# Five of seven block products of two spans in a second level of Strassen, and the later norms' roots by logarithm and exponential

## The chip, the cores and the metric

The kernel runs on one core of a Trainium2 chip. The metric is device time in microseconds (us) of one execution; lower is better. The engines are TensorE (PE, with its weight loads listed as PEld), VectorE (DVE), ScalarE (ACT), GpSimd (POOL) and SyncE (SP), which issues most DMAs. Each works through its own instructions in the order in which the program lists them; semaphores hold an instruction until what it needs is there.

## The reference: what is computed

Attention with normalised queries and keys, then a feed-forward block, all in float32. Sizes: batch 8, 12 heads, 448 positions, head size 64; so 3584 tokens of 768, and a hidden size of 2048.

```python
def rmsnorm(x, g):
    rms = np.sqrt(np.mean(x * x, axis=-1, keepdims=True) + 1e-06)
    return x / rms * g
scores = scale * np.matmul(rmsnorm(q, g_q), rmsnorm(k, g_k).transpose(0, 1, 3, 2))
attn = np.exp(scores - max); attn = attn / (sum + 1e-9)
x = np.matmul(attn, v)            # -> tokens x 768
h = x @ w_in                      # 768 -> 2048
out = (np.maximum(h, 0.0) ** 2) @ w_out   # 2048 -> 768
```

## The kernel before, in words

**Spans.** Two batches make a span; there are four (NSPAN). The attention of span 0 runs first, alone (`attention_alone`, L917). Then each span has its first product (`first_product`, L1034: x @ w_in and the activation) and its second product (g @ w_out). Spans 0, 1 and 2 use `second_product` (L1091), span 3 uses `last_product` (L1144).

**Strassen.** Both products of a span are done in one level of Strassen over the two batches and the two halves of each dimension: seven block products instead of eight, named A11, A12, S2, S1, S3, A22, S4. The seven sums of weights are made once and kept in DRAM (`w1s`, `w2s`). The seven sums of activations are made by `combine` (L1021) into `gC` and `gT`, and by `combine_x` (L903) into `xC` and `xT`. One block product of the second product has 3 blocks of 128 output rows (m = 0 to 2, HC), a depth of 8 times 128 (HF), and 448 columns (S): 24 matmuls of 128x128 by 128x448. The hardware profile keeps two records for each of these float32 matmuls. `last_product` already splits the first two row blocks of each block product by a second level of Strassen: seven half-size products, each 4 matmuls by 224 columns, and the third row block is done plainly.

**Order around the change.** The order of every engine is written by hand. `attention(first)` (L972) and `second_product` are generators. The loop at L1379 runs one attention step and then draws so many units from `second_product` (`total`, `done`, L1378 to L1382); a unit is one matmul of `second_product`. An attention pair (two heads; 12 pairs per span) has five steps, each ended by a `yield`:

- A (L976 to L996): scores of two key chunks, the values of the pair before, the other two scores (all PE work of a pair is here), exponentials on ACT, `add_up` 1 and `norm_by_squares(i + 2)` on DVE and POOL;
- B (L997 to L1001): `transposes(i + 1)` (DVE), the load of v;
- C (L1002 to L1009): `add_up` 2 and 3, `finish(i - 1)` (DVE), `squares(i + 3)` (ACT);
- D (L1010 to L1014): `fold(i)` (DVE), `combine_x(i - 1)` (POOL, for the span's second batch);
- E (L1015 to L1018): POOL issues the DMA of the sums' reciprocals to DRAM and the two that spread them over partitions (`spread`, L826).

`norm_by_squares` (L739) sums squares on DVE (L744), swaps neighbouring groups of 32 partitions by four small DVE copies (L747), and takes the power -1/2 on POOL (L750), which then scales q and k (L752). `fold` (L812) sums the exponentials (L817) and moves quarters by three small DVE copies (L820).

**PSUM.** There are eight banks. `scores` holds four (`ps_s`), `values` two (`ps_o`), and two are left to the products (`ps_m`): `bank()` (L460) hands them out in turn, so `second_product` fills one bank while DVE or ACT reads the other. `last_product`, which has no attention beside it, keeps its sums pa, pb, pc and pd in four different banks.

**Weights.** `load_blocks` (L651) streams weight tiles `sw` in the order of use, five buffers ahead, on SP's queue.

## Time and profile before

| what | value |
|---|---|
| runs | 1353.47 us median of 3 (1352.96, 1353.47, 1356.8) |
| the profiled execution | 1352.32 us, of which the span of its instructions is 1350.1 us |
| busy share of the span | PE 98%, PEld 50%, DVE 65%, POOL 46%, ACT 32% |
| granted TensorE clock | 0.999 |
| second products of spans 0, 1, 2, with attention | 265.0 to 457.7, 587.0 to 778.9, 908.0 to 1100.0 us |
| first products of spans 0 to 3 | 131 to 265, 457.7 to 587.0, 778.9 to 908.0, 1100 to 1226 us |
| last product | 1226 to 1350 us |

How to read it: a line such as L1106 is a line of the kernel. A group's mean in ns is the length of one record; matmuls overlap in the pipeline, so a row of matmuls is paced by the distance of their starts, which is shorter than one record. Idle time of an engine costs something only where the chain that ends last runs through it.

### The profile page before, as it was taken

The page shows a single profiled execution, that of the slowest core. Times are in us where ns is not written, and L with a number is a line of the kernel's source. Part 1 is how long each engine was busy: PE and PEld are TensorE (multiplying, and loading weights), DVE is VectorE, ACT ScalarE, POOL GpSimd, SP SyncE. Part 2 cuts the span into 40 slices and gives each one's busy share as a digit, 9 for nine tenths or more (in the row PEclk, how much of TensorE's full clock was granted, in tenths as well). Part 3 has the DMA queues.
Part 4 walks back from the last instruction along what each step waited for, and adds up shares of the span by engine and source line. Part 5 has one row for each costly group of instructions (what it writes and reads, how often), then busy time and mean ns, then how long its engine had stood idle before and what let it go on. Part 6 is the DMA issues. An engine that isn't in the chain of part 4 may idle for free.

```text
span 1350.1 us, 17275 instructions
## 1 busy us (share of the span) xinstructions
PE 1329.7 (98%) x5786; PEld 671.6 (50%) x5786; DVE 873.4 (65%) x1537; ACT 431.8 (32%) x681; POOL 619.4 (46%) x504
## 2 busy tenths in 40 slices
PE   8999999999999999999999999999999999999997
PEld 3333445444444455444444455544444445556887
DVE  6999788599987333568777623457878743336553
ACT  7886466433332011233333111223333201111000
POOL 5767533466564122646556212446656412422452
PEclk9999999999999999999999999999999999999999
DMA  9877999655686333345676432345665444431333
GB/s 241 225 217 200 314 360 333 181 131 107 135 151 129 101 87 88 101 114 114 143 146 123 114 97 87 90 112 125 130 123 126 105 102 135 134 88 53 114 101 58
DMA packets 413814, 190.15 MB, mean 141 GB/s; under 512 B 282388, under 2 KB 408724, under 8 KB 413716
## 3 DMA queue, kind: packets, MB, share of 16 engines
q1 hardware_dynamic: 406164, 180.21, 52.0%
q0 software_dynamic: 4736, 8.40, 2.4%
q8 instruction: 48, 0.79, 0.3%
q10 hardware_dynamic: 2816, 0.34, 0.2%
q14 instruction: 50, 0.41, 0.1%
HBM read 155.72 MB, written 33.16 MB: 140 GB/s over the span
## 4 chain that ended last, share of the span: by engine, by line
PE 89%; DVE 5%; ACT 2%; DMA 1%; issue 1%; POOL 0%; SPq 0%; POOLq 0%; DVEq 0%
PE ps L1106 29%; PE pd L1068 10%; PE pa L1068 10%; PE pc L1068 10%; PE sc L785 7%; PE pav L862 7%; PE pb L1068 5%; PE ps L1234 3%; PE pd L1206 2%; PE pc L1206 2%; PE pa L1206 2%; DVE gT L810 1%; PE pb L1206 1%; DVE rstd L715 1%; ACT gT L797 1%
## 5 line engine op out<-in xcount | busy, mean ns | idle before, releaser
L1106 PE MATMUL ps<-gT,sw 128*128 128x448 f32 x576 | 225.8, 543 | 0.0
L1044 POOL TENSOR_TENSOR gT<-gT 128x448 f32<-128x448 f32 x96 | 94.1, 982 | 284.8 <-ACT gT L1040 284.8
L750 POOL TENSOR_TENSOR half<-half,mhalf 128x28 f32<-128x28 f32 x36 | 175.3, 4869 | 74.6 <-DVE half L749 74.0
L1106 PE MATMUL ps<-gC,sw 128*128 128x448 f32 x432 | 170.1, 543 | 0.0
L1106 PEld LDWEIGHTS ps<-gT,sw 128*128 128x128 f32 x576 | 107.5, 190 | 113.9 <-issue 110.1
L1068 PE MATMUL pa<-xT,sw 128*128 128x448 f32 x384 | 155.0, 540 | 0.6 <-ACT p L1072 0.6
L1040 ACT ACTIVATE gT<-gT 128x448 f32<-128x448 f32 x96 | 55.3, 576 | 313.4 <-DVE gT L1083 313.4
L1106 PEld LDWEIGHTS ps<-gC,sw 128*128 128x128 f32 x432 | 80.6, 190 | 86.3 <-issue 83.2
L787 ACT ACTIVATE pr<-sc 128x896 f32<-128x896 f32 x87 | 77.5, 915 | 124.1 <-PE sc L785 124.1
L785 PE MATMUL sc<-qkT 64*64 64x448 f32 (+1 forms) x1152 | 109.8, 496 | 0.0
L1068 PEld LDWEIGHTS pa<-xT,sw 128*128 128x128 f32 x384 | 72.8, 190 | 72.7 <-issue 70.1
L583 POOL TENSOR_TENSOR gC<-gC 128x384 f32<-128x384 f32 x64 | 76.2, 1208 | 62.2 <-DVE gC L579 60.4
L1083 DVE TENSOR_TENSOR gT<-z,pd 128x448 f32<-128x448 f32 x32 | 19.8, 619 | 97.8 <-PE pd L1068 97.7
L1068 PE MATMUL pd<-xT,sw 128*128 128x448 f32 x192 | 77.9, 542 | 1.3 <-DVE z L1075 1.3
L1068 PE MATMUL pd<-xC,sw 128*128 128x448 f32 x192 | 77.5, 540 | 1.3 <-DVE gT L1083 1.3
L830 POOL DMA_DIRECT2D xT<-factors x72 | 38.0, 532 | 88.4 <-DMA factors<-square 56.8
L1068 PE MATMUL pb<-xC,sw 128*128 128x448 f32 x192 | 77.5, 540 | 0.1
L1068 PE MATMUL pc<-xC,sw 128*128 128x448 f32 x192 | 77.4, 539 | 0.0
L1068 PE MATMUL pc<-xT,sw 128*128 128x448 f32 x192 | 77.4, 539 | 0.0
L752 POOL TENSOR_TENSOR qk<-qk,half 128x448 f32<-128x448 f32 x72 | 75.9, 1074 | 2.8
L862 PE MATMUL rest<-pr,vt 64*64 64x448 f32 x348 | 72.7, 537 | 0.0
L862 PE MATMUL pav<-pr,vt 64*64 64x448 f32 x348 | 72.7, 537 | 0.0
(233 smaller groups left out, 2159.2 us busy)
## 6 DMA issues: line engine op xcount, KB each, us to landing
sw<-w1s SPq DMA_DIRECT2D x224, 192.0 KB, 2.4
sw<-w2s SPq DMA_DIRECT2D x126, 256.0 KB, 3.3
w1s<-gC SPq DMA_DIRECT2D x8, 1344.0 KB, 7.1
w2s<-gC SPq DMA_DIRECT2D x8, 1344.0 KB, 6.3
out_dram<-osb SPq DMA_DIRECT2D x184, 56.0 KB, 1.8
qk<-in_q_dram SPq DMA_DIRECT2D x144, 56.0 KB, 3.4
qk<-in_k_dram SPq DMA_DIRECT2D x144, 56.0 KB, 2.8
xT<-factors POOLq DMA_DIRECT2D x72, 112.0 KB, 3.4
```

Of the source, the lines that this page charges most:

```text
L583: nc.gpsimd.tensor_tensor(*[blocks_of(n)[:, place_of(n, i)] for i in (dst, x, y)], op)
L750: nc.gpsimd.tensor_tensor(half, half, mhalf, ALU.pow)
L752: nc.gpsimd.tensor_tensor(qkn[:, s], raw[:, s], half[:, s * NG:(s + 1) * NG].rearrange("p g -> p g ()").to_broadcast([P, NG, 32]), ALU.mult)
L785: nc.tensor.matmul(sc[part, h, 0:n], qkT[rows, 0, 1, keys], qkT[rows, 0, 0, of], start=True, stop=True)
L787: nc.scalar.activation(pr, sc[:, :, 0:n], AF.Exp)
L862: nc.tensor.matmul(into, vs[i][rows, h, c, :], probs[i, c][rows, h, :], start=(c == 0), stop=(c == NF), skip_group_check=True)
L1040: nc.scalar.activation(g, src, AF.Relu)
L1044: nc.gpsimd.tensor_tensor(g, g, g, ALU.mult)
L1068: nc.tensor.matmul(ps, stream[n + at][:, c], rhs[:, c], start=first and c == 0, stop=c == HC - 1, skip_group_check=not first)
L1106: nc.tensor.matmul(ps, stream[n][:, c % 4], rhs_of[i][:, c], start=c == 0, stop=c == HF - 1)
L1206: nc.tensor.matmul(ps, lhs[:, c], rhs[:, c], start=first and c == 0, stop=c == HK - 1, skip_group_check=not first)
L1234: nc.tensor.matmul(ps, weights_of(o, m, c // HK)[:, c % HK], rhs_of[i][:, c, part], start=c == 0, stop=c == HF - 1)
```

## The change

1. **Second products of spans 1 and 2** use a new generator, `outer_product`, in place of `second_product`. A11 and A12 stay as they are. In S2, S1, S3, A22 and S4 the first two row blocks go through a second level of Strassen, and the third is done in two column halves of 224 (`third`). The sums of activations for the second level (`add_g`, four of 128x896 per block product) go on DVE, those of weights (two in `add_weights`, and two changes of a11 and a12 in place) on POOL. A unit is now two matmuls by 224 columns or one by 448, and `total` is 140 in place of 160.
2. **PSUM.** The second level needs four sums, and two banks are there: `held` cuts each bank into two halves of 224 columns. pa and pb lie in one bank and pc and pd in the other. pc and pd are open at once; only the first matmul into pc has the start flag, which clears the bank for both.
3. **Norms after span 0's.** The power on POOL gives way to Ln and Exp on ACT and four small POOL operations (`roots_by_squares`). The copies of `norm_by_squares` and `fold` move from DVE to ACT, and what follows them is put into functions of its own that are called a step later (`scale_by_squares` in step B, `roots_by_squares` in step C, `factors_of` in step E).
4. The order of weight loads becomes a list made at the start (`plan`, `begins`). The weights of the second level are loaded in four tiles per block product into dead parts of xC, xT and gC (`load_set`).

```diff
+    plan, begins = [], {}
...
     def norm_by_squares(i):
...
-            nc.vector.tensor_copy(other[n * 32:(n + 1) * 32], half[m * 32:(m + 1) * 32])
+            nc.scalar.copy(other[n * 32:(n + 1) * 32], half[m * 32:(m + 1) * 32])
...
+    def roots_by_squares(i):
...
-        nc.gpsimd.tensor_tensor(half, half, mhalf, ALU.pow)
+        nc.scalar.activation(y, half, AF.Ln, scale=2.0 ** -63)
+        nc.scalar.activation(y, y, AF.Exp, scale=-0.5, bias=rebias)
+        nc.gpsimd.tensor_tensor(half, half, y, ALU.mult)
+        nc.gpsimd.tensor_tensor(half, half, y, ALU.mult)
+        nc.gpsimd.tensor_scalar(half, half, -0.5, 1.5, ALU.mult, ALU.add)
+        nc.gpsimd.tensor_tensor(half, half, y, ALU.mult)
...
     def fold(i):
...
-            nc.vector.tensor_copy(quarters[0:32, n], quarters[n * 32:(n + 1) * 32, 0])
+            nc.scalar.copy(quarters[0:32, n], quarters[n * 32:(n + 1) * 32, 0])
+
+    def factors_of(i):
...
+    def outer_product(work, span):
...
+        order = (A11, A12, S2, S1, S3, A22, S4)
...
+        def add_g(o, k):
+            if o < len(order):
+                (b11, b12), (b21, b22) = [[b.rearrange("p (r h) n -> p r h n", h=2) for b in row] for row in parts_of(o)]
+                t1, t2, t3, t4 = (t_of(o, k) for k in range(4))
+                dst, x, y = ((t1, b12, b11), (t2, b22, t1), (t3, b22, b12), (t4, b21, t2))[k]
+                nc.vector.tensor_tensor(dst, x, y, sub)
+
+        def add_weights(o):
+            if o < len(order):
+                a11, _, a21, a22, s1 = tiles[o]
+                nc.gpsimd.tensor_tensor(s1, a21, a22, add)
+                nc.gpsimd.tensor_tensor(a21, a11, a21, sub)
+
+        def run(ps, lhs, rhs, start=True):
+            for c in range(HK):
+                nc.tensor.matmul(ps, lhs[:, c], rhs(c), start=start and c == 0, stop=c == HK - 1, skip_group_check=True)
+                if c % 2:
+                    yield
...
+        held = [ps[:, h * HS:(h + 1) * HS] for ps in (bank("both"), bank("both")) for h in range(2)]
+        for o, i in list(enumerate(order))[2:]:
...
+            pa, pb = held[o % 2], held[1 - o % 2]
+            pc, pd = held[2], held[3]
...
+            def third(half, ps):
+                for c in range(HF):
+                    load_blocks(n + 5)
+                    nc.tensor.matmul(ps, stream[n + c // 4][:, c % 4], rhs_of[i][:, c, half],
+                                     start=c == 0, stop=c == HF - 1, skip_group_check=True)
+                    if c % 2 and c < HF - 1:
+                        yield
+                nc.vector.tensor_tensor(dst[2][:, half], base[2][:, half], ps, add)
+                if more is not None:
+                    nc.vector.tensor_tensor(more[2][:, half], more[2][:, half], ps, add)
+                yield
+
+            yield from run(pa, a11, of(b11))
+            nc.scalar.copy(z, pa)
+            nc.gpsimd.tensor_tensor(a11, s1, a11, sub)
+            if o != 5:
+                send(o)
+            if o == 2:
+                add_g(2, 3)
+            else:
+                add_g(o + 1, 0)
+            yield from third(left, pc)
+            load_set(o + 1 if o > 2 else len(order))
+            yield from run(pa, a12, of(b21), False)
+            nc.gpsimd.tensor_tensor(a12, a12, a11, sub)
+            send(o)
+            if more is None:
+                nc.vector.tensor_tensor(into[0][:, left], base[0][:, left], pa, add)
+            else:
+                nc.scalar.copy(into[0][:, left], pa)
+            add_g(o + 1, 1 if o > 2 else 0)
+            yield from run(pb, a11, of_t(t2))
+            nc.vector.tensor_tensor(z, z, pb, add)
+            if more is None:
+                nc.gpsimd.tensor_tensor(into[1][:, left], z, base[1][:, left], add)
+                nc.gpsimd.tensor_tensor(into[0][:, right], z, base[0][:, right], add)
+            yield from run(pc, s1, of_t(t1))
+            nc.vector.tensor_tensor(y, z, pc, add)
+            yield from run(pd, a21, of_t(t3), False)
+            if more is None:
+                nc.vector.tensor_tensor(into[1][:, right], base[1][:, right], pd, add)
+                nc.gpsimd.tensor_tensor(into[1][:, right], into[1][:, right], y, add)
+            else:
+                nc.vector.tensor_tensor(into[1][:, right], y, pd, add)
+            add_g(o + 1, 2 if o > 2 else 1)
+            yield from third(right, pa)
+            n += 2
+            add_weights(o + 1)
+            if leaves:
+                deliver(work, span, dst[2], 2 + col, t)
+            yield from run(pc, a12, of(b22), False)
+            nc.vector.tensor_tensor(into[0][:, right], into[0][:, right] if more is None else z, pc, add)
+            add_g(o + 1, 3 if o > 2 else 2)
+            yield from run(pd, a22, of_t(t4), False)
+            nc.vector.tensor_tensor(into[1][:, left], into[1][:, left] if more is None else z, pd, add)
...
+            if i + 2 < last:
+                scale_by_squares(i + 2)
...
+            if i + 2 < last:
+                roots_by_squares(i + 2)
...
+                factors_of(i)
                 nc.gpsimd.dma_start(sums["out"][i % 2], sums["square"][0:2 * S // 32, 1])
...
-            rest = second_product(work, span)
+            rest = (outer_product if span else second_product)(work, span)
...
-            total, done, most = HC * (7 * HF + 4) - 20, 0, 10 * NPAIR + 1
+            total, done, most = 2 * HC * HF + 5 * 22 - 18 if span else HC * (7 * HF + 4) - 20, 0, 10 * NPAIR + 1
```

## The prediction, made before the changed kernel ran

> **What bounds the kernel now.** I read the chain that ended last first, then the table by stage, then PE, DVE and POOL in order of time. The chain is PE from end to end:
>
> ```profile
> PE 89%; DVE 5%; ACT 2%; DMA 1%; issue 1%; POOL 0%; SPq 0%; POOLq 0%; DVEq 0%
> ```
>
> By stage (start:end, length; then busy us of PE, PEld, DVE, ACT, POOL), the second products of spans 1 and 2, which the change rewrites:
>
> ```profile
> 587.00:778.90 191.90, 191.90 (x1088) 89.88 (x1087) 145.41 (x286) 58.49 (x82) 99.03 (x75) 1.00 0.59 126
> ...
> 908.00:1100.00 192.00, 192.00 (x1088) 89.97 (x1087) 144.76 (x286) 58.47 (x82) 99.33 (x75) 1.00 0.55 120
> ```
>
> PE is busy in all of it, DVE in 76%, POOL in 52%. So fewer matmul columns shorten these stages as long as PE never has to wait there; a shorter POOL or ACT alone gains nothing. How the attention lies in it (PE in order of time, span 1):
>
> ```profile
> 643.64 1.73 PE L785 MATMUL sc<-qkT 64*64 64x448 f32 x16
> ...
> 647.82 1.31 PE L785 MATMUL sc<-qkT 64*64 64x224 f32 x16
> 649.06 9.29 PE L1106 MATMUL ps<-gC,sw 128*128 128x448 f32 x24
> ...
> 659.03 1.73 PE L785 MATMUL sc<-qkT 64*64 64x448 f32 x16
> ```
>
> A pair's PE work is one lump, 643.64 to 649.06 = 5.42 us, then only product matmuls until the next lump at 659.03: a pair takes 15.4 us. The second level exists already in span 3; PE there:
>
> ```profile
> 1244.25 6.18 PE L1234 MATMUL ps<-gT,wb 128*128 128x448 f32 x16
> 1250.26 1.68 PE L1206 MATMUL pb<-xT 128*128 128x224 f32 x8
> 1251.78 1.68 PE L1206 MATMUL pc<-xT 128*128 128x224 f32 x8
> ...
> 1260.96 6.18 PE L1234 MATMUL ps<-gC,qk 128*128 128x448 f32 x16
> ```
>
> 16 records by 448 columns take 6.01 us from start to start (0.3757 each), 8 by 224 take 1.515 (0.1893 each).
>
> **PE work saved.** A float32 matmul leaves two records. A block product now: 24 x 2 x 0.3757 = 18.03 us. After: seven half products of 4 matmuls and a third block of 16, 44 x 2 x 0.1893 = 16.66. Saved 1.37, ten times (five products, two spans): **13.7 us**. The product of span 3 above took 16.71, so this pace can be had. Floor: 1352.3 (the profiled execution's own time; its span is 1350.1) - 13.7 = 1338.6.
>
> **Norms and copies.** Per pair POOL loses the power (L750, mean 4869 ns) and gains four operations on 28 columns. The trace has none: from below DVE's 188 ns (L748), from above POOL's 658 ns by 224 columns (L1255), so 0.7 to 2.6 us. DVE loses seven copies (4 at 174, 3 at 339 ns, 1.7 us); ACT gains them at 0.17 to 0.53 us each (L747; L992) and Ln and Exp (216 and 307 ns, L725, L726): 1.7 to 4.2 us per pair, with ACT busy 58 of 192 us. PE does not wait in span 0's second product either (busy 192.70 of 192.70), so nothing of this is on the path: 0, at best 0.8 (192.7 against 191.9). Weight loads: the same bytes, SP's queue, no row of PE waiting for `sw` in these stages: 0. What ACT's copies can cost: they wait in ACT's order for a DVE sum, and the exponentials stand behind them; `fold`'s copies come some 4.6 units (3.5 us) before the next lump, and PE has 2.6 us of values before it needs the first exponential, so DVE has to be some 6 us late; from then on its lateness would be paid.
>
> **DVE.** Attention per pair from its rows: adds 2 x 1.06 + 2 x 0.65 (L810, L808), sums 1.10 + 1.08 (L817, L744), two transposes 1.23 (L761), `finish` 0.62 + 0.66, and 1.2 of small ones: 9.3 us. In the middle four products (S2 to A22, 88 units of a matmul's length each): 17 `add_g` at 1.08 (L1192 where alone), 33 reads of a 224-wide sum at 0.385 (L1276, L1280), 5 transposes out at 0.64: 34.3 us. The loop draws 140 units over 61 steps, 11.5 per pair: 4.5 us. Together 13.8 us per pair against PE's 11.5 x 0.757 + 5.42 = 14.1. Busy times are 4% under the sum of the rows (145.4 against 151 in this stage), so 13.3. DVE fits, but 11 of it falls outside the lump, where PE takes 8.7: DVE runs up to 3 us late there, and catches up in the lump.
>
> POOL also slows DVE. From DVE and POOL in order of time:
>
> ```profile
> 1270.46 1.29 POOL L1180 TENSOR_TENSOR xT<-wb 128x512 f32<-128x512 f32 x1
> 1270.51 2.19 DVE L1192 TENSOR_TENSOR xT<-gC,xT 128x896 f32<-128x896 f32 x1
> 1271.33 1.51 PEld L1206 LDWEIGHTS pa<-gC,qk 128*128 128x128 f32 x8
> 1271.51 1.68 PE L1206 MATMUL pa<-gC,qk 128*128 128x224 f32 x8
> 1271.82 2.00 POOL L1180 TENSOR_TENSOR xT<-xT,wb 128x512 f32<-128x512 f32 x1
> ```
>
> The DVE add doubles beside POOL's. Over the last product L1192 averages 1.35 against 1.08 (+25%, POOL busy 41%). But L900 (two inputs in SBUF) stays at 0.62 beside L752. DVE has 6.5 us per pair of such adds: 0 to 1.6 us more; I take 0.3, as most of them are attention's, whose rows did not grow. The Trainium skill (GPSIMD Engine Reference, section Specifications) says that POOL's SBUF interfaces are shared with VectorE and that instructions with two SBUF inputs contend. By that rule all 6.5 us would grow, and the sum would move toward the upper end of this range; L900 says not every pair of operations does.
>
> **The new wait.** pa and pb share one bank, pc and pd the other. Three times per product the next matmuls write the half beside one just finished: pb after pa, pd after pc, and pd after pc again. Before the matmuls may start, DVE has to read that half, if accesses of two engines to one bank are kept in program order whatever the columns. Before has no two sums in one bank, so the trace does not show this. From below 0. From above, the nearest row, a matmul that waits until DVE has read its bank (span 2's first product):
>
> ```profile
> 863.82 0.61 DVE L1075 TENSOR_TENSOR z<-p,pb 128x448 f32<-128x448 f32 x1
> ...
> 864.49 0.30 PEld L1068 LDWEIGHTS pd<-xT,sw 128*128 128x128 f32 x2 [0.63 <-DVE z L1075]
> ```
>
> The read ends at 864.43 and PE resumes within 0.06 to 0.15 us. Read starts come 0.20 us after PE could have gone on (1320.04 and 1320.24, L1206 and L1280). So one wait is 0.20 + 0.39 + 0.1 = **0.7 us with an idle DVE**, plus all that stands before the read in DVE's queue. I take the wait: that row is the nearest, and the framework that places the semaphores orders an engine's access to a bank behind another's. The Trainium skill (PSUM — Partial Sum Buffer, section on bank collisions) says that two engines on one bank and quadrant at once raise an error even at disjoint columns, and that semaphores are to guard whole banks. With that rule the upper bound holds; without it, the lower. The one clearing flag itself removes no instruction: 0.
>
> **One product by hand**, steps A to E as the loop places them, PE's lump at 0. S2: lump to 5.4; units 1 to 8 would end at 11.5. DVE: step A's add waits for the second exponential (2.8 after the lump's start), two operations, 5.0; B 1.5; transpose out and `add_g` 1.7; C 3.6; third block's read 0.4; D 1.1; then the read of pa, done at 13.7: PE stands **2.3** us. The next wait (pd after pc) comes after the second lump, DVE is prompt: **0.7**. After it DVE has B, a read, `add_g`, C, a read, D, E and the read of pc ahead of PE's next start, 9.3 us of work and 0.3 of waiting for PE, against eight units of PE, 6.1: **3.7** with the restart. Sum 6.7. S1, shifted by a step: 2.4, 0 (the lump covers it), 2.8: 5.2. Mean 6.0, times four products and two spans: 48. S4 has no `add_g` and mostly no attention: 3 x 0.7 x 2 = 4. Off for overlapping rows, 0.5 us per pair (1 per product): -8. Contention 0.3 per pair: 0.6 x 8 = +5. Waits together 49, less 13.7: **+35**. So 1352.3 + 35 = 1387.6 for the profiled execution; its median of runs lies 1.15 higher (1353.47 against 1352.32): **1389**.
>
> **Rivals.**
> *Prompt DVE.* Only the bare waits: 0.7 x 3 x 10 = 21, less a few under lumps, 19; -13.7: 1359. For it: DVE is 24% idle now. Against: 13.3 of 14.1 us when it matters.
> *No wait within a bank: faster.* Reads of one half do not hold the other half, or the lumps cover them; then the shortest cover is four units (3 us) and DVE is mostly in time: 1340 to 1349. It decides at 13.7 / 30 = 0.46 us per wait, under the 0.7 of an idle DVE. At or near that point the time is unchanged.
> *DVE and POOL hold each other.* Contention of 1.6 us per pair (2.5 more per product, 8 products: +20) and a11 late from POOL, whose queue stands behind DMA landings (17.7 us of waits in span 1): 1405 to 1425.
> *The change does not do what it says*: at 224 columns a weight load (190 ns) is as long as the matmul's step, so PE cannot go below 0.1893; at 0.1878 it would save 14.9 in place of 13.7. That is in the sum.
>
> **Numbers.** Forecast, waits of 4 to 8 us per product (1374 to 1404): 0.52. Prompt DVE (1355 to 1374): 0.16. Held by contention (above 1404): 0.18. No or covered wait: 0.10 faster, 0.04 unchanged. A change under 0.3% can't be told from none here. Range 1357 to 1413: the forecast, nearly all of the prompt case, half of the contention. Faster 0.10, same 0.04, slower 0.86.
>
> **What would show it.** Right: in the second products of spans 1 and 2 PE is idle before the runs into pb and pd, some 24 us per span, and what ended it are DVE's reads of pa and pc; each stage is about 191.9 - 6.9 + 24.5 = 209.5 us long; S2 to A22 take 22 x 0.757 + 1.9 lumps of 5.42 + 6 = 33 us each; 224-wide records start 0.189 us apart. POOL's power is gone, and span 0's second product still takes 192 us. Wrong: PE busy throughout in these two stages (no such wait), or idle there with POOL, ACT or a DMA as what ended it, or starts further apart than 0.19.

## The result, and the profile after

The changed kernel takes 1460.39 us (median of 4 runs, 1459.51 to 1468.63), the kernel before 1354.28 (4 runs): 1.0795 times as long, 95% interval 1.0752 to 1.0837. The forecast was 1389 and the range 1357 to 1413: the sign was right, the loss three times the one forecast (106 us for 35).

Read in the same order as before. The changed kernel's row of granted clock in 40 slices, and its chain:

```profile
PEclk9999999999999999998998999999898899999999
...
PE 77%; DVE 12%; ACT 3%; issue 3%; DMA 2%; SPq 1%; POOL 1%; DVEq 0%; POOLq 0%; ACTq 0%
```

The path now runs through DVE for 12%, and the clock drops in two stretches. They are the second products of spans 1 and 2. By stage (start:end, length; PE, PEld, DVE, ACT, POOL; granted clock):

```profile
588.90:832.20 243.30, 203.67 (x1292) 138.07 (x1289) 162.37 (x252) 82.83 (x185) 119.47 (x143) 0.92 0.44 98
961.90:1203.90 242.00, 203.23 (x1292) 137.53 (x1289) 161.73 (x252) 82.88 (x185) 119.68 (x143) 0.92 0.41 94
```

Each takes 50 us more than its 192.7 of before; of a profiled difference of 107.9 us (1460.23 against 1352.32) the two hold 99.8. DVE is busy in only two thirds of them. Cut finer, span 1:

```profile
588.50:631.00 42.50, 42.50 (x248) 19.50 (x244) 29.30 (x48) 22.94 (x52) 15.84 (x26) 1.00 0.66 154
...
660.00:681.00 21.00, 16.70 (x112) 12.34 (x112) 13.46 (x22) 7.23 (x17) 10.44 (x15) 0.91 0.24 48
681.00:702.00 21.00, 17.30 (x108) 12.73 (x109) 14.49 (x25) 7.49 (x17) 9.18 (x12) 0.83 0.49 120
...
811.00:832.90 21.90, 20.29 (x119) 17.02 (x118) 8.61 (x20) 0.88 (x2) 6.13 (x9) 1.00 0.30 61
```

A11 and A12 (first line) lose nothing, S2 to A22 lose idle time and clock, S4 (last line, no attention beside it) hardly anything. PE in order of time, in S2 of span 1; the bracket is the idle time before, and what ended it:

```profile
672.47 3.19 PE L1295 MATMUL both<-gC,sw 128*128 128x224 f32 x16
675.50 1.68 PE L1229 MATMUL both<-gC,xC 128*128 128x224 f32 x8
682.04 3.36 PE L1229 MATMUL both<-gT,xC 128*128 128x224 f32 x8 [4.87 <-DVE p L1343]
685.19 1.33 PE L1229 MATMUL both<-gC,xC 128*128 128x224 f32 x3
```

The second run into pc ends, and the run into pd waits 4.87 us for DVE's read of pc (L1343), as forecast in place. But then its eight records take 3.36 us where the eight before took 1.68: the clock is at half. What DVE did meanwhile:

```profile
666.73 1.09 DVE L832 TENSOR_TENSOR acc<-pr 128x896 f32<-128x896 f32 x1 [3.20 <-ACT pr L809]
...
670.41 0.39 DVE L1329 TENSOR_TENSOR xC<-xC,both 128x224 f32<-128x224 f32 x1 [1.59 <-PE both L1229]
670.72 1.16 DVE L783 STREAM_TRANSPOSE qkT<-qk 128x448 f32<-128x448 f32 x2
...
673.98 1.55 DVE L832 TENSOR_TENSOR acc<-acc,qkT 128x896 f32<-128x896 f32 x1
675.57 1.27 DVE L830 TENSOR_TENSOR acc<-acc,half 64x448 f32<-64x448 f32 x2
676.87 0.62 DVE L926 TENSOR_TENSOR half<-pav,half 128x448 f32<-128x448 f32 x1
677.52 1.21 DVE L928 TENSOR_TENSOR xT<-half,xT 128x448 f32<-128x448 f32 x1
...
680.80 0.33 DVE L849 TENSOR_REDUCE square<-quarters 32x28 f32<-32x112 f32 x1 [0.75 <-ACT quarters L842]
...
681.65 0.33 DVE L1343 TENSOR_TENSOR p<-p,both 128x224 f32<-128x224 f32 x1
```

In the lump before (first line) it had stood itself, 3.20 us for an exponential. It waited for PE (1.59 us), then did one pair's attention steps B to E in a row, and only then the read of 0.33 us for which PE stood. DVE's waits in this stage (us in all, times, longest):

```profile
DVE acc L832 <- ACT pr L809: 25.3, 7, 4.6
DVE ct L1299 <- PE both L1295: 12.0, 5, 5.1
DVE acc L832 <- ACT qkT L809: 7.0, 2, 4.1
```

32 us of this stage DVE waits for exponentials, in the lumps; in the kernel before it is 18.7 us in the same stage, and PE never waits. So PE and DVE **take turns**: DVE idles in the lump, PE behind it. Every span has 14 waits of PE, 39.6 and 38.7 us: three in each of S2, S3, A22 and S4, two in S1. Eight are long (2.7 to 6.4), six are near the bare wait for one read (0.48 to 0.57).

### The profile page after: what moved, and what is told of

The parts are those of the page before. It is cut to its first block, busy times and chain, and to the rows that moved or that the text cites. A ratio compares the mean times of both kernels' runs of the same rounds, so it can differ in the third digit from the quotient of the medians.

```text
span 1458.4 us, 18435 instructions
## 1 busy us (share of the span) xinstructions
PE 1354.4 (93%) x6186; PEld 768.5 (53%) x6186; DVE 883.6 (61%) x1371; ACT 507.7 (35%) x1017; POOL 610.3 (42%) x684
## 4 chain that ended last, share of the span: by engine, by line
PE 77%; DVE 12%; ACT 3%; issue 3%; DMA 2%; SPq 1%; POOL 1%; DVEq 0%; POOLq 0%; ACTq 0%
PE pd L1104 10%; PE pa L1104 9%; PE pc L1104 9%; PE ps L1142 8%; PE both L1229 7%; PE sc L807 7%; PE pav L890 6%; PE ps L1243 5%; PE pb L1104 5%; PE ps L1460 3%; PE both L1295 2%; PE pd L1432 1%; DVE acc L832 1%; PE pa L1432 1%; PE pc L1432 1%
## 5 line engine op out<-in xcount | busy, mean ns | idle before, releaser
L1229 PE MATMUL both<-gT,gC 128*128 128x224 f32 x288 | 75.0, 417 | 45.0 <-DVE gC L1319 12.8
L1229 PEld LDWEIGHTS both<-gT,gC 128*128 128x128 f32 x288 | 64.0, 229 | 55.0 <-POOL xC L944 12.3
L842 ACT COPY quarters<-quarters 32x28 f32<-32x28 f32 x108 | 22.9, 212 | 164.4 <-DVE quarters L839 162.8
L1142 PE MATMUL ps<-gT,sw 128*128 128x448 f32 x192 | 75.3, 543 | 0.0
L769 POOL TENSOR_TENSOR half<-half,other 128x28 f32<-128x28 f32 x36 | 18.0, 499 | 136.6 <-ACT other L768 131.2
L1243 PE MATMUL ps<-gT,sw 128*128 128x448 f32 x192 | 74.8, 544 | 0.0
```

The source lines that it names most:

```text
L1142: nc.tensor.matmul(ps, stream[n][:, c % 4], rhs_of[i][:, c], start=c == 0, stop=c == HF - 1)
L1229: nc.tensor.matmul(ps, lhs[:, c], rhs(c), start=start and c == 0, stop=c == HK - 1, skip_group_check=True)
L1243: nc.tensor.matmul(ps, stream[n][:, c % 4], rhs_of[i][:, c], start=c == 0, stop=c == HF - 1)
```

## The experiments

Stage lengths are from the first matmul of a second product to the first of the next first product; idle is PE's gaps over that stage, both from PE's rows in order of time. Ratios are to the kernel before on the same chip.

| kernel | us (runs) | ratio [95%] | stages, span 1 and 2 | PE idle |
|---|---|---|---|---|
| before | 1354.28 (4) | 1 | 192.7, 192.7 | 0, 0 |
| after | 1460.39 (4) | 1.0795 [1.0752, 1.0837] | 243.2, 242.0 | 39.6, 38.7 |
| e1 norms only | 1353.83 (10) | 1.0009 [0.9999, 1.0019] | 192.7, 192.7 | 0, 0 |
| e2 old norms | 1490.84 (1) | | 259.8, 259.1 | 51.7, 51.6 |
| e3 four banks | 1438.78 (4) | 1.0632 [1.0615, 1.065] | 230.2, 235.7 | 29.8, 30.1 |
| e4 busy waits | 1438.26 (1) | | 234.0, 232.3 | 12.0, 11.5 |
| e5 no activation sums | 1450.31 (1) | | 236.4, 238.8 | 36.6, 37.0 |
| e6 no weight sums | 1460.43 (1) | | 242.7, 242.4 | 37.7, 37.1 |
| e7 reads at once | 1446.76 (4) | 1.0684 [1.0666, 1.0702] | 236.9, 235.7 | 33.1, 33.5 |
| e8 alternate banks | 1405.08 (4) | 1.0365 [1.0346, 1.0383] | 217.4, 213.0 | 21.1, 20.5 |
| e9 attention re-spread | 1423.47 (4) | 1.0527 [1.0506, 1.0548] | 224.4, 221.6 | 26.5, 25.2 |
| e10 both | 1379.96 (4) | 1.0192 [1.0172, 1.0211] | 203.7, 200.0 | 11.8, 8.2 |
| e11 longer cover | 1427.01 (4) | 1.053 [1.0507, 1.0552] | 221.5, 222.7 | 23.4, 25.4 |
| e12 cover, re-spread | 1400.32 (4) | 1.0359 [1.0322, 1.0395] | 208.0, 207.1 | 15.1, 16.0 |
| e13 every read covered | 1366.96 (6) | 1.0106 [1.0089, 1.0123] | 197.5, 196.9 | 8.5, 8.1 |
| e14 covered, old attention | 1375.78 (4) | 1.0168 [1.0153, 1.0182] | 202.4, 199.6 | 11.0, 10.7 |
| e15 late readers mended | 1353.18 (12) | 0.9998 [0.9988, 1.0008] | 191.4, 190.1 | 4.6, 3.2 |
| e16 norm moved | 1353.61 (12) | 1.0003 [0.9993, 1.0012] | 191.7, 190.2 | 4.9, 3.4 |
| e17 values read earlier | 1354.29 (12) | 0.9999 [0.9989, 1.001] | 191.9, 190.0 | 4.1, 2.5 |
| e18 power in first norms | 1350.63 (11) | 0.9981 [0.9972, 0.999] | 191.7, 190.7 | 5.0, 3.5 |

### e1 and e2: which part of the change

```diff
# e1: part 3 alone
-            rest = (outer_product if span else second_product)(work, span)
+            rest = second_product(work, span)
...
# e2: part 3 undone
-        nc.gpsimd.tensor_tensor(half, half, y, ALU.mult)
...
+        nc.gpsimd.tensor_tensor(half, half, mhalf, ALU.pow)
```

> Part 3 alone: norms by logarithm and exponential and the copies on ACT, but all three spans keep the plain second product with its two alternating banks. If the loss comes from waits between sums in one bank (theory), PE has no wait here and the time is that of before: 1350 to 1358 us, with PE busy over 99% in all three second products. If the copies on ACT and the round trips between DVE and ACT cost PE by themselves (rival), it is above 1370 us.

> The second level of Strassen with the norms and copies of before (power on POOL, copies on DVE), so part 3 undone. Theory: DVE has 1.7 us more per pair in front of the reads, and POOL 3 us more in front of a11, so the waits grow: 1460 to 1490 us. Rival (the moved copies make DVE wait for ACT, and that is the loss): 1400 to 1435 us.

Part 3 alone adds 1.3 us by its medians (1353.83 against 1352.54), and its interval takes in none; without it the new product is 30 us slower still (one run). The loss is the product's, and part 3 softens it.

### e3: the sums in four banks

```diff
-        held = [ps[:, h * HS:(h + 1) * HS] for ps in (bank("both"), bank("both")) for h in range(2)]
+        both, narrow[0] = two_banks("both"), two_banks("sc")
+        held = [bank("both")[:, 0:HS], both[:, 0, 0:HS], bank("both")[:, 0:HS], both[:, 1, 0:HS]]
```

> The changed kernel with pa, pb, pc and pd in four different banks. The two more banks come from the scores, which in this part have two banks, one per head, with an exponential per head; the values are split around the second chunk of scores, and two product units lie before the last scores, so that PE need not wait for the exponentials. Theory (a sum's read holds the matmuls into the other half of its bank): PE's idle time of 39 us per span falls under 10 and the 224-wide records go back to 0.19 us: 1345 to 1375 us. Rival (DVE and POOL have too much work, wherever the sums lie): idle stays above 30 us per span and the time above 1420 us.

A fifth of the loss went, not all. What PE waits for in span 1 (us, times, longest):

```profile
PE both L1248 <- DVE p L1366: 6.5, 1, 6.5
PE both L1248 <- DVE xC L1366: 6.3, 1, 6.3
```

L1366 reads pd. The runs that wait write the pa of S1 and of A22, which is the other bank of the same two-bank buffer; that bank's own sum had been read long before. So the buffer as a whole was kept in order, and this run took less away than it meant to. The waits moved to other points and stayed long. Its time is the rival's (above 1420), but as the buffer still tied the sums together it decides nothing between the two.

### e4: the clock

```diff
+            def keep_busy():
+                if o < 6:
+                    idle = ps_o.tile([P, S], F32, tag="t", name="idle")
+                    for _ in range(5):
+                        nc.tensor.matmul(idle, rhs_of[i][:, 0, 0:P], rhs_of[i][:, 0], start=True, stop=True)
...
+            keep_busy()
             yield from run(pb, a11, of_t(t2))
```

> The changed kernel with five matmuls for nothing (3.8 us) ahead of the first and the third wait of S2, S1, S3 and A22, into a bank of the attention that is free then. They add 60 us of PE work in all and no result. If the clock granted after a long wait is what stretches the 224-wide records from 0.19 to 0.31 us (theory: 19 us per span), the clock stays at full and the time falls by 20 to 35 us, to 1425 to 1440 us, though PE has more to do. If the records are long for another reason, the time stays or grows: 1455 to 1480 us.

PE does 3.8 us of work for nothing ahead of 16 waits, 60 us in all, and the kernel is 22 us faster (one run). The mean granted clock goes from 0.971 to 0.994. Filled-in and remaining idle time are 42 us per span, more than after's 39; the gain is the clock's.

### e5 and e6: less work for VectorE, less for GpSimd

```diff
# e5, in add_g
-            if o < len(order):
+            if o < 3:
# e6, in add_weights, and the same for a11 and a12
-            if o < len(order):
+            if o < 3:
```

> Leaves out the second-level sums of activations of S1, S3, A22 and S4 (16 of 20 per span, about 17 us of VectorE's work per span; stale data is multiplied). Theory (each of the eight long waits per span is VectorE's lateness at one point: what stands ahead of the read in its queue, less TensorE's cover; one such sum, 1.1 to 1.5 us, stands ahead of most of these reads): each long wait falls by 1 to 2 us, 10 to 16 us per span with the clock's loss on top, 1415 to 1440. Rival (VectorE's total work is what is too much, and all of it is paid): 34 us of work and most of the clock's loss go, 1395 or less. Second rival (VectorE's own work is not what is late; it waits for ScalarE and GpSimd): above 1445.

> Leaves out GpSimd's sums of weights of S1, S3, A22 and S4 (16 of 20 operations of 128x512 per span, about 20 us of GpSimd's work per span; unsummed weights are multiplied). Theory of the queue: GpSimd only lengthens VectorE's adds beside it; 20 us overlap with two-input adds for a third of the time at a loss of 0.4, some 3 us per span: 1445 to 1460. Rival (GpSimd is what is late, as the page's lines that name it say): the long waits fall by half or more, 1420 or less.

In span 1's stage DVE is busy 20.5 us less in e5 (141.9 for 162.4), which buys 3 to 7 us per stage; POOL is busy 23.8 us less in e6 (95.6 for 119.5), which buys nothing (each ran once). Neither engine's amount of work is most of what PE waits for. For e5 my size was too large; its time is the second rival's case, and what DVE waits for in the changed kernel is above all the exponentials of the lump.

### e7 and e8: when a sum is read, and what covers the read

```diff
# e7
-                if c % 2:
+                if c % 2 and c < HK - 1:
                     yield
...
             nc.vector.tensor_tensor(z, z, pb, add)
...
+            yield
# e8, beside it: order pa, third left, pa, pd, pb, pc, third right, pd, pc
-            pa, pb = held[o % 2], held[1 - o % 2]
-            pc, pd = held[2], held[3]
+            pa, pb, pc, pd = held[o % 2 * 2:] + held[:o % 2 * 2]
```

In both, a part of S3's first output block is overwritten before it is sent; in e8 (and e10) one of the second level's terms is missing from one quarter of each product, with the same number of instructions.

> Same work, same order on TensorE. Each sum's read is put into VectorE's queue in the same draw as the sum's last matmuls, so ahead of an attention step that falls between. Theory of the queue: a step falls there for some four in ten of the reads and holds 1.9 us of VectorE's work on average: the long waits fall by 0.8 us on average, 6 to 10 us per span, 1435 to 1455. Rival (VectorE has no time to spare, so what no longer stands ahead of one read stands ahead of the next): within 5 us of 1460.

> Same work, reads put in as in the run before it. TensorE's order is changed so that no run of matmuls writes the bank whose sum was just finished: pa, third block's left half, pa, pd, pb, pc, third block's right half, pd, pc, with the banks changing places in each product. Every read then has the next run in the other bank as cover, at least two matmuls by 448 columns, 1.5 us. Theory (sharing a bank sets only where lateness is paid, and each long wait is 2.7 to 6.4 us): each of the waits shrinks by 1.5 us and the bare ones of 0.5 go, some 15 us per span, and 5 to 10 of the clock's: 1405 to 1430. Rival (the shared bank itself is the cause): no waits are left, 1340 to 1360.

Both as the theory had it (e8 at the near end of its range). Cover is what PE can do in the other bank while a read is still to come. 1.5 us of cover at every read takes half of the loss; reading at once alone, an eighth.

### e9 and e10: the attention's steps placed otherwise

```diff
+            if i > first + 1:
+                scale_of(i - 2)
+                combine_x(i - 2)
+            if after:
+                fold(i - 1)
                 values(i - 1)
...
-                add_up(i, 2)
-                add_up(i, 3)
-            if i > first:
-                finish(i - 1)
+                add_up(i, 2)
...
+            yield
+            if here:
+                add_up(i, 3)
...
+            yield
+            if after:
+                sum_of(i - 1)
```

> The changed kernel with the attention's small steps placed otherwise, the products untouched: the fold of the pair before and its last multiplication go to the start of the lump, where VectorE waits for exponentials; the reciprocals go to the step behind the lump, the two adds of exponentials to two steps, the sum of the values to a step of its own. Same operations. Theory (TensorE and VectorE take turns: VectorE idles in the lump and has nearly all its attention work in one row behind it, where each shared bank makes TensorE wait for it): of 9.3 us behind a lump 2.6 go into it, so each long wait falls by some 2 us, 15 us per span, and half of the clock's loss: 1405 to 1430. Rival (VectorE has too much work in all, wherever it stands): 1450 to 1465.

> The re-spread attention together with the order of the products that changes banks at every run (each sum read in the draw of its last matmuls). Theory of the turns: 1.5 us of cover at every wait on top of the re-spread: waits of 5 to 10 us per span are left, hardly any clock loss: 1350 to 1375. Rival (too much work): the two gains are the same gain, 1395 to 1405 as with the banks alone.

The same operations, some moved into the lump and the rest to other steps, gain 37 us, and with e8's order 80. Alone the two gain 37 and 55, together 80 of these 92, so the rival of e10 falls; e10 stays 5 us above its range.

### e11 to e14: one read without cover

```diff
+            yield from run(pa, a12, of(b21), False)
...
+            yield from run(pb, a11, of_t(t2))
+            nc.vector.tensor_tensor(z, z, pb, add)
...
+            tail = third(right, pb, n, i, dst, base, more, (col, t) if leaves else None)
+            for _ in range(3):
+                next(tail)
+                yield
...
# e13 and e14, in third: the tail's matmuls, then (after the next run into pa) its read
+                if late:
+                    load_blocks(n + 7)
+                    yield
```

> The changed kernel's attention, with a third order of the products: pa and pb are read behind the third block's left half and the second run into pa, pc and pd together behind the third block's right half, of which a quarter is kept for behind the last two runs. Every read now has at least three units, 2.3 us, of matmuls in the other bank as cover. Theory (turns): against the alternating order with 1.5 us of cover another 0.8 to 1.5 us goes from each of its eight waits per span, 22 us of idle in a span become 10 to 14, with the clock's loss 1375 to 1392. Rival (waits only move): within 5 us of 1405.

> The same order of the products with the re-spread attention, in which the last multiplication (which waited for a DMA for 19 us of a span, ahead of the fold) now stands behind the first add of exponentials. Theory (turns): idle of 14 and 8 us in the two spans falls to under 5 each, no clock loss: 1348 to 1362; the floor is 1338.6 and about 2 us per span are lost at the start of the next first product to late weights. Rival (VectorE's adds beside GpSimd, up to twice as long, set a bottom that no order removes): 1368 to 1380.

> As the run before with the re-spread attention, but the third block's last read is put behind the next run into pa, and the weights of the next blocks are asked for ahead of the output's DMAs. Each sum's read now has at least two units (1.5 us), mostly three to four, of matmuls in the other bank ahead of the next run into its own. Theory (lateness at points without cover): the one wait per product that was left (2.7 to 5.1 us, 14.5 us per span) and its clock loss go, and the 3.7 us at the start of the next first product: 1345 to 1358. Rival (VectorE slowed beside GpSimd sets a bottom): 1370 or more.

> The same order of the products with the changed kernel's own attention. Theory: VectorE is up to 6 us late there behind a lump, cover is 1.5 to 3 us, so 1 to 3 us at some four points per span are left with some clock loss: 1360 to 1385. Rival (the one read without cover was all that was left): within 8 us of the run before. Rival (too much work): 1400 or more.

e11 and e12 missed, by my own order: the third block's last quarter and the next pa share a bank, and its read stood between them. That made the pair e11 and e14 the clearest run of the study. They differ in the place of that read, and in the weights' loads being asked for ahead of the output's DMAs. PE in e11:

```profile
675.04 0.92 PE L1297 MATMUL both<-gC,sw 128*128 128x224 f32 x4
682.15 1.86 PE L1229 MATMUL both<-gC,xC 128*128 128x224 f32 x4 [6.18 <-DVE p L1301]
683.94 3.26 PE L807 MATMUL sc<-qkT 64*64 64x448 f32 x16
```

and in e14, at the same point:

```profile
674.51 0.92 PE L1298 MATMUL both<-gC,sw 128*128 128x224 f32 x4
675.26 0.92 PE L1229 MATMUL both<-gC,xC 128*128 128x224 f32 x4
676.12 1.73 PE L807 MATMUL sc<-qkT 64*64 64x448 f32 x16
```

One read per product without cover cost 6.18 us there, and then half clock (1.86 for 0.92, 3.26 for 1.73). Without it the stages are 19.1 and 23.1 us shorter; 11.5 us more (5.1 and 6.4) come from the next first products, whose weights e11 had late. With the changed kernel's own attention and all of its work, e14 is 85 us faster than the changed kernel: 22 of the 106 us of loss are left. DVE's busy time in span 1's stage is 162.9 us (162.4 in the changed kernel), but it now waits for exponentials there only this long:

```profile
DVE acc L832 <- ACT qkT L809: 5.1, 2, 2.8
...
DVE acc L832 <- ACT pr L809: 4.3, 2, 2.5
```

9.4 us for 32: both engines stopped taking turns. The rival that DVE has too much work falls. The other one, that the uncovered read was all that was left, falls narrowly: e14 is 8.8 us behind e13, where it allowed 8. e13 is 9 us above its range, short of its rival's 1370.

### e15: the rest

In e13, one of the last waits of PE (2.66 us) stood for a read by DVE, which itself waited for a copy by ACT of the other sum in the same bank:

```profile
684.79 0.39 DVE L1324 TENSOR_TENSOR p<-p,both 128x224 f32<-128x224 f32 x1 [2.92 <-ACT xC L1332]
```

```profile
680.97 0.54 ACT L809 ACTIVATE half<-sc 128x448 f32<-128x448 f32 x1 [5.11 <-DVE xT L917]
...
684.41 0.35 ACT L1332 COPY xC<-both 128x224 f32<-128x224 f32 x1
```

ACT's copy was late because an exponential before it waited for a buffer that DVE still read (L917). e15 gives that buffer a third copy, puts the third block's read ahead of ACT's copy and GpSimd's four sums later; it also moves the last multiplication to the end of step A, sends one output later and keeps one output buffer in place of two. What each of these is worth was not taken apart.

```diff
-tag=f"half{m}", name="half", bufs=1) for m in range(2)]
+tag=f"half{m}", name="half", bufs=1) for m in range(3)]
...
-            nc.scalar.copy(z, pa)
             if tail:
                 next(tail)
+            nc.scalar.copy(z, pa)
...
+            for those, x, m in adds:
+                nc.gpsimd.tensor_tensor(those[m], x[m], blocks[m], add)
```

> As the run with every read covered and the re-spread attention, with a third buffer for the half chunk of exponentials (so that ScalarE's exponential no longer waits for the last multiplication, and its copy of pa not behind it), the third block's read put ahead of that copy, and GpSimd's four sums at the end of S3 put behind its sum of weights for A22. Theory: the waits of 2.7, 1.2 and 3.3 us per span go, with 1 to 2 us of the clock's: 14 to 17 us off 1367, so 1349 to 1355, as fast as before or a little faster. Rival (VectorE and GpSimd beside each other set a bottom, other points turn late): 1360 or more.

Within its range, 1353.18, and no different from before. Its stages (191.4 and 190.1) are now shorter than one level's 192.7, at full clock:

```profile
587.40:778.80 191.40, 186.76 (x1292) 128.69 (x1289) 156.26 (x248) 83.86 (x185) 112.79 (x143) 1.00 0.56 125
908.20:1098.30 190.10, 186.85 (x1292) 128.51 (x1289) 161.84 (x251) 83.87 (x185) 115.32 (x143) 1.00 0.52 119
```

PE's 186.8 us busy is the forecast floor, 192.74 - 6.85 = 185.9, within 0.9.

### e16 to e18: the norms' own price

```diff
# e16: behind the last exponentials of the attention alone
-                norm(NAT)
+                squares(NAT)
...
+                norm_by_squares(NAT)
+                scale_by_squares(NAT)
+                roots_by_squares(NAT)
# e17, beside it, in step D; step E takes add_up(i, 3)
-            if here:
-                add_up(i, 3)
+            if after:
+                sum_of(i - 1)
# e18, from e15: the first two later norms as before the change
+            nc.gpsimd.tensor_tensor(half, half, mhalf, ALU.pow)
```

In e16 and e17 a later load overwrites the queries and keys of the first later norm before they are scaled.

> As the run at parity, with the first later norm's copies, logarithm and exponential put behind the last exponentials of the attention alone. Theory (ScalarE waited 2.7 us there for VectorE with exponentials behind it): the first product of span 0 starts 2 to 3 us earlier, 1349 to 1352. Rival (the start varies from kernel to kernel for other reasons): within 1.5 us of 1353.2.

> As the run before it, and the sum of the values (VectorE's read of the bank that the next pair's values need) a step earlier, ahead of the last add of exponentials. Theory: the waits of 1.3 to 1.7 us before the values, 2.7 to 3.2 us per span, go: another 4 to 6 us, 1344 to 1348, faster than before. Rival (VectorE is then late elsewhere): no gain over the run before.

> As the run at parity, with the two norms that lie in the attention alone and in span 0's first product made as before (copies on VectorE, power on GpSimd); all other norms by logarithm and exponential. Theory (the copies and what waits for them cost 2 to 3 us there): the first product of span 0 starts at 132 to 133 us instead of 134.4, 1350 to 1352. Rival (the start varies for other reasons): within 1.5 us of 1353.2.

e16 gained nothing: PE's 1.17 us wait for an exponential at the end of the attention alone became one of 2.27 for DVE's read of a sum, behind the same copies. e17 took the values' waits away and PE found others; no gain either. In e15 the last stretch before the first product (from the three `tot` sums, 124.49, to 134.37) takes 9.88 us; in e16 11.82; in e18 (125.86 to 133.53) 7.67, the same as before (124.61 to 132.28). The kernel e2, with the old norms, also takes 7.67 there, and the changed kernel 9.88. So the norms by logarithm cost 2.2 us at that one place, where ACT waited for DVE with exponentials behind it:

```profile
126.29 0.88 ACT L752 COPY other<-half 32x28 f32<-32x28 f32 x4 [2.73 <-DVE half L749]
127.71 0.23 ACT L767 ACTIVATE other<-half 128x28 f32<-128x28 f32 x1 [0.53 <-DVE half L758]
```

That these 2.2 us are all of e18's gain is not shown. Its first product starts at 133.53, outside the 132 to 133 expected and only 0.84 ahead of e15's, as the `tot` sums themselves came 1.37 later; between the two profiled executions (2.28 us) span 2's first product makes 1.4, with 1.2 us of late weights in e15 and none in e18, and the last product 1.3, less 1.2 elsewhere. e18 is faster than the kernel before, by 0.1 to 0.28% (less than the 0.3% that the forecast held to be the least that can be told from none), and faster than the changed one by some 110 us.

## Why the prediction was wrong, step by step

Two steps failed: the hand schedule made PE's waits too short, and the clock's loss behind them was no term of the sum.

- **What bounds, and the floor**: right. PE bound the two stages; the saving of 6.85 us per stage is there once PE is fed (e15).
- **The new wait**: right in kind and in place: 14 waits per span, each at one of the three points named. Bare it is 0.48 to 0.57 us, not 0.7. The Trainium skill (PSUM — Partial Sum Buffer, section on bank collisions) advises to guard by bank; every one of these waits, and e11 against e14, agrees that order is kept by bank here, and e3 showed a coarser order, by buffer.
- **The hand schedule failed in size.** Forecast per span 24.5 us, measured 39.6 and 38.7. In span 1, S2 was 2.3 + 0.7 + 3.7 and is 4.46 + 0.48 + 4.87; S1 5.2 and is 6.8; S3 and A22 were given the mean of these two, 6.0, and are 11.0 and 10.4; S4 2 and is 1.6. In S2's second long wait DVE was to need 9.6 us from the lump to the end of the read and took 11.3 (670.72 to 681.98): adds beside POOL at 1.55 and 1.21 in place of 1.06 and 0.66, and waits for PE and for ACT's copies, which part 3 put into DVE's order. The 1.21 is the operation that the prediction expected to stay at 0.62 beside POOL. Over both spans this term is 78.3 - 49 = 29 us.
- **The clock had no term.** In the two stages PE is busy 203.7 and 203.2 us, with the same number of records that take 186.8 and 186.9 at full clock in e15: 33 us. With it, 78.3 of idle time + 33 - 13.7 = 98 of the 99.8 us. "Records start 0.189 apart" was the sign named, and it failed: 3.36 us for eight records.
- **Contention** at 0.3 us per pair: too small at one point, A22's first wait, where one add of DVE took 4.3 us longer beside POOL (2.5 in span 2; lines below); over a whole pair not settled. Without POOL's sums of weights (e6) DVE is busy 3.9 us less in span 1's stage (158.5 for 162.4) and A22's first wait falls to 4.20 us, but S2's first grows from 4.46 to 5.05 and PE's busy time by 1.3, and the time stays; what POOL's other work adds to DVE's attention rows was not taken out. The rival that had DVE and POOL hold each other came nearest in time (1405 to 1425), but of its two prices the late a11 is refuted by e6, and the other is this open one.
- **DVE as nearly full (13.3 of 14.1 us per pair)**: the sum was fair, the use of it not. Full or not did not decide (e5, e14); that its work lay behind the lump with nothing covering the reads did. DVE did not catch up in the lump, as the prediction had it: it waited there for exponentials.
- **Norms and copies at nothing**: 2.2 us at one place (e18), +1.3 us in all by medians (e1).
- The other 8.1 us of 107.9 lie outside the two stages: 3.3 at the start (the norms' 2.2 among it), 3 in the first products of spans 2 and 3 (weights late, a term that the prediction put at 0), 2.5 in the last product (cause not tried).

The waits of S3 and A22 were longer than those of S2 and S1. For S3's first, 5.54 us, the traces show what held it. ACT's copy of pa (L1321) stood behind the copies of `fold`, which part 3 had moved to ACT and which waited for DVE:

```profile
740.92 0.69 ACT L842 COPY quarters<-quarters 32x28 f32<-32x28 f32 x3 [4.38 <-DVE quarters L839]
741.51 0.33 ACT L1321 COPY xC<-both 128x224 f32<-128x224 f32 x1
```

In e7, which puts the copy into ACT's queue ahead of that step, it waits for PE alone, and PE's wait there is 0.53 us (the next one, bare in the changed kernel, is 3.75):

```profile
731.00 0.35 ACT L1320 COPY xC<-both 128x224 f32<-128x224 f32 x1 [0.31 <-PE both L1229]
```

For A22's first wait (6.39 us, 5.24 in span 2) they show it too: of the adds ahead of DVE's read of pa one took 5.39 us, where its median is 1.09. It ran beside POOL's four sums at the end of S3 (L1352) and one of weights (L1306), and ended 0.95 us after them:

```profile
773.38 5.39 DVE L832 TENSOR_TENSOR acc<-pr 128x896 f32<-128x896 f32 x1 [4.37 <-ACT pr L809]
...
774.37 2.22 POOL L1352 TENSOR_TENSOR p<-p,xC 128x448 f32<-128x448 f32 x2
776.56 1.26 POOL L1306 TENSOR_TENSOR gC<-gC 128x512 f32<-128x512 f32 x1
```

In span 2 it took 3.61 us and in e6, without L1306, 3.00, and both times it ended 0.95 to 0.96 us after POOL's last. Of DVE's adds of 128x896 in after and e2 to e15, behind the first 150 us, 29 took over 2.4 us, and 28 of them ended 0.95 to 0.96 us after the end of an operation of POOL. e15 has these four sums later. No run moved them alone.

## What to carry to other kernels

Before two sums share a bank, list every read that stands between two runs of matmuls into it, and give each one the work of another bank as cover; one read per product left out cost 42 us here (e11 against e14, the two stages). What a wait costs is the reader's lateness at that moment, not the read's length and not its engine's share of busy time, and a bunch of other work behind a stretch in which that engine idled is what made it late here. Add the clock's price to PE waits of 2 us and more: some 1.7 us (an estimate, half of a stretch of 3.41 us at half clock, see below).

## What the hardware showed beyond that

Behind PE's waits of 2.7 us and more the granted clock was mostly half: eight records by 224 columns took 3.15 to 3.36 us in place of 1.68. But the length of the wait does not decide. A wait of 2.66 us was followed by half clock in span 1 of the changed kernel:

```profile
696.26 1.68 PE L1229 MATMUL both<-gC,xC 128*128 128x224 f32 x8
700.60 3.15 PE L1229 MATMUL both<-gT,xC 128*128 128x224 f32 x8 [2.66 <-POOL qk L774]
```

and by full clock in e13:

```profile
685.23 1.78 PE L1248 MATMUL both<-gC,xC 128*128 128x224 f32 x8 [2.66 <-DVE p L1324]
```

The same wait in span 2 of the changed kernel (2.65 us, ended at 1073.84) was also followed by full clock. Behind a wait of 2.05 us in e14 the next four records took 1.02 us, as in full clock, behind one of 2.06 in e10 the next eight took 3.05.

What decides is how the idle time falls on a grid. In these traces the granted clock changes, while the kernel runs, only at points of a fixed grid of 3.41 us (each trace has its own offset). The changed kernel around its two waits, cut on that grid (as by stage above: start:end, length; PE first, granted clock third from the end):

```profile
697.38:700.79 3.41, 0.75 (x4) 0.43 (x4) 3.35 (x7) 0.53 (x3) 3.15 (x6) 1.00 0.58 161
700.79:704.20 3.41, 3.41 (x10) 3.09 (x10) 1.87 (x5) 0.11 (x1) 2.40 (x2) 0.50 0.68 110
1069.43:1072.84 3.41, 1.76 (x10) 1.41 (x8) 3.28 (x7) 1.10 (x2) 2.84 (x5) 1.00 0.90 236
1072.84:1076.25 3.41, 2.41 (x13) 2.44 (x14) 3.06 (x7) 0.64 (x3) 3.40 (x4) 1.00 0.48 81
1076.25:1079.67 3.42, 3.42 (x33) 1.63 (x35) 0.00 (x0) 1.59 (x2) 1.36 (x4) 1.00 0.40 66
```

The first wait lies inside one stretch of the grid, in which PE is busy 0.75 us, and the next stretch has half clock. The second is cut in two (busy 1.76 and 2.41), and the clock stays full. Counted by PE's rows, from 18 us on, in the twenty traces (before, after, e1 to e18): of the stretches of full clock in which PE idled less than 1.85 us, none of 7653 was followed by half clock; of those with more than 2.05 us, all 131; in between, 12 of 26.

The Trainium skill (TensorE: Matmul & The Clock Gate, Part 1 on the HAM clock gate) has the clock fall to half after an idle window of about 3.4 us, by a window that runs freely. The grid agrees with the free window; but a window did not have to be idle throughout, some 2 us of idle time within it were enough here.
